# mLSTM attention and mixer on one core: four of twelve spread products move between the heads' products with v

## The chip, the cores and the metric

The kernel runs on one core of a Trainium2 chip. The metric is the device time of one execution in microseconds. The kernel before takes 427.3 us (median of three runs, 426.74 to 427.36).

## The reference

Two parts follow each other. The first is an mLSTM attention for 4 batches, 8 heads, 768 steps, head width 40:

```python
m_new = np.maximum(f_gate[:, :, t] + m, i_gate[:, :, t])
f_stab = np.exp(f_gate[:, :, t] + m - m_new)
i_stab = np.exp(i_gate[:, :, t] - m_new)
C = f_stab * C + i_stab * np.einsum('bhd,bhe->bhde', vt, kt)
n = f_stab * n + i_stab * kt
h_tilde = np.einsum('bhde,bhe->bhd', C, qt)
denom = np.maximum(np.abs((n * qt).sum(-1)), 1.0)
y[:, :, t] = sigmoid(o_gate) * h_tilde / denom
```

The second is a mixer on the heads put side by side (768 tokens of 320 channels in each batch): `h = relu(xT @ w_tok1) @ w_tok2`, `u = x + hT`, and the output is `u + relu(u @ w_ch1) @ w_ch2`, with 256 token units and 1536 channel units. Everything is float32.

## The kernel before, in words

The 768 steps of a batch are cut into 6 chunks of 128. A unit is one chunk of one batch, written (b, c), with all 8 heads. Inside a unit the recurrence is a masked attention: products of q and k (`st_s`, line 313), multiplied on VectorE with a matrix of decays (`st_p`, line 323), then for each head a product with v (`st_pv`, line 439). What came before the chunk enters by the running state (`st_state`, lines 378 and 386). Then the sigmoid gate, the division, and the mixer's matmuls follow.

The matrix of decays is the exponential of phi(t) + b(s), and of a large negative number above the diagonal. Both rows are first computed on VectorE, with one row for each head, in the tile `z` (phi in its first half, b in its second). For the first batch alone, TensorE spreads these rows into full matrices in PSUM, in two halves of four heads. A half is a PSUM bank of 128 x 512 and takes six bf16 products: one 512-column product that writes the mask (`spread_late`, line 165), four 128-column products that spread phi, one for each head (line 180), and one 512-column product that spreads b over the four heads (line 183). The two halves of a unit so hold four long products and eight thin ones. ScalarE then takes the exponential of each half (`prep_exp`, line 291). In bf16 the rows of `z` stand in three parts whose sum is the float32 value. The lower two are made by `split`, two subtractions, for chunks 0 to 2 on VectorE, and for chunks 3 to 5 in one go on GpSimd (lines 174 and 175). Every spread product of a chunk reads all three parts.

The banks come from the PSUM pool `ps_h`, which has two buffers, handed out in turn. A third user of that pool is `spread_q` (line 198, with the two small products of lines 138 and 139): it spreads phi for the scaling of q, and ScalarE reads its bank in `prep_q3` (line 274, an exponential) and right behind it in `cols_w0_out` (line 142).

The loop over the first batch's chunks, c = 1 to 5, is written by hand, and every engine runs its instructions in the order in which they are written. For c up to 3, one turn issues on TensorE: `st_s` of unit c+1, `spread_q` of unit c+1, `st_state` and `st_pv` of unit c, and then the two spread halves of unit c+2. So in each turn `spread_q` takes one buffer of `ps_h`, the first half takes the other, and the second half takes the one that `spread_q` had. On ScalarE one turn issues, among steps that unpack the mixer's weights (lines 684, 654, 658) and a rounded copy of the output (line 490): line 274, line 142, then the two exponentials of line 291. The weights arrive by DMAs that SyncE issues (line 643), between the loads of k and v (line 247) and q (line 258).

The long loops behind it (mixer matmuls of lines 696, 817 and 843, and the attention of batches 1 to 3, which does not spread by TensorE) are left as they are.

Of the kernel before, what the change touches and what calls it, by code (L numbers as in the profile page):

```python
# [17 lines left out]
B, H, S, D = 4, 8, 768, 40  # L18
L = 128
# [16 lines left out]
def kernel(ctx: ExitStack, tc: tile.TileContext, gates, qk, q3, kv, og,  # L36
                            wt1, wt2, wc1, wc2, ident, out):
    nc = tc.nc
# [4 lines left out]
    ps_h = ctx.enter_context(tc.tile_pool(name="ps_h", bufs=2, space=PSUM))  # L43
# [31 lines left out]
    z = pp.tile([128, 2, S], F32, name="z")  # L75
# [23 lines left out]
    id3 = pp.tile([128, HP], BF16, name="id3")  # L99
# [11 lines left out]
    phi, b_t = z[0:B * HP, 0], z[0:B * HP, 1]  # L111
# [51 lines left out]
    def spread_late(pool, tag):  # L163
        ps = pool.tile([128, 4, L], F32, tag=tag, name="ps_phi")
        nc.tensor.matmul(ps, id_b, late_b.unsqueeze(1).to_broadcast([128, 4, L]), start=True, stop=False)
        return ps


    def top(x):
        return x.bitcast(BF16).rearrange("... (t i) -> ... t i", i=2)[..., 1]  # L170
# [6 lines left out]
    def spread_phi(r, c, h0=0, h1=H):  # L177
        zc = top(z[:, :, c * L:(c + 1) * L])
        for h in range(h0, h1):
            nc.tensor.matmul(r[h // 4][:, h % 4, :], id3[:, h:h + 1].to_broadcast([128, 128]),  # L180
                             zc[:, 0], start=False, stop=False)
            if h % 4 == 3:
                nc.tensor.matmul(r[h // 4], zc[:, 1], id3[:, h - 3:h + 1].unsqueeze(2).to_broadcast([128, 4, L]),
                                 start=False, stop=True)

    def spread_split(u, fill=0):
        T[u]["phi"] = r = []
        for h in range(0, H, 4):
            r.append(spread_late(ps_h, "h"))
            if fill and h == 0:  # L190
                warm(fill)
            spread_phi(r, u[1], h, h + 4)

    def spread_q(u, pool=(ps_h, "h")):
        b, c = u
        ps = pool[0].tile([128, 512], F32, tag=pool[1], name="ps_q")
        for g in range(3):
            nc.tensor.matmul(ps[0:120, g * L:(g + 1) * L], sel3[:, g],
                             top(z[:, 0, c * L:(c + 1) * L]), start=True, stop=True)
        T[u]["psq"] = ps[0:120, 0:3 * L].rearrange("p (g t) -> p g t", g=3)  # L200
        if c < NC - 1:
            T[u]["psw"] = ps[:, 3 * L:3 * L + HP]
            cols_w0(T[u]["psw"], c)


    T = {}
# [25 lines left out]
    def load_phi(u):  # L232
        b, c = u
        T.setdefault(u, {})
        third = b < 2 and c % 3 == 2
        dd = ap.tile([128, H, L], F32, tag="p12" if third else "dd", name="dd", bufs=1 if third else 2)
        if b:
            nc.sync.dma_start(out=dd, in_=phi_d[c, b * HP:b * HP + H].partition_broadcast(128))
        T[u]["dd"] = dd
# [67 lines left out]
    def st_s(u, mult=True, mid=iter(()), rows=64, pool=(ps_s, "s")):  # L307
        t = T[u]
        t["s"] = [pool[0].tile([128, 4, L], F32, tag=pool[1], name="ps_sc") for _ in range(2)]
        for h in range(4):  # L310
            for hf in range(2):
                r = t["raw"][64 * hf:64 * hf + rows]
                nc.tensor.matmul(t["s"][hf][:, h, :], r[:, 1, h, :], r[:, 0, h, :], start=True, stop=True)  # L313
        if mult:
            st_p(u, mid)
# [105 lines left out]
        if not joined(u):  # L421
            st_state(u, (ps_s, "s"))

    def st_pv(u, copy=True):
        b, c = u
        t = T[u]
        vx = t["kv"][:, DM:]
        if "p" in t:
            return st_pv3(u)
        if c:  # L430
            po = t["po"]
        else:
            t["bank"] = ps_m.tile([128, 512], F32, tag="m", name="po")
            po = t["bank"][:, 0:H * E1].rearrange("p (h e) -> p h e", e=E1)
        for h in range(H):
            o, x = po[:, h, :], vx[:, h * E1:(h + 1) * E1]
            if b == 0 and c:
                o, x = po[:, 0:h + 2:h + 1, :], x.unsqueeze(1).to_broadcast([128, 2, E1])
            nc.tensor.matmul(o, t["dd"][:, ROW[h], :], x, start=c == 0 and h == 0, stop=h == H - 1)  # L439
        if b == 0 and c:  # L440
            po = po[:, 1:1 + H]
        t["po"] = po
        if b:
            st_ht(u)

    def st_ht(u):
        t = T[u]
        po = t["po"]
        ht = ap.tile([128, H, E1], F32, tag="ht", name="ht", bufs=1)
        nc.scalar.activation(ht, po, AF.Copy)  # L450
        t["ht"] = ht
# [431 lines left out]
    def step(g, n=1):  # L883
        for _ in range(n):
            next(g, None)

    def warm(n, pool=(ps_m, "m"), z=zero):
        t = pool[0].tile([128, 512], F32, tag=pool[1], name="warm")
        for i in range(n):
            nc.tensor.matmul(t[:, 0:z.shape[-1]], z[:, 0:128], z, start=i == 0, stop=i == n - 1)  # L890
# [76 lines left out]
    for c in range(1, NC):  # L967
        u, n1, n2, n3 = (units[c + i] for i in range(4))
        if c == 1:
            st_s(n1)  # L970
        elif c < NC - 1:
            dg = dec_ops(0)
            st_s(n1, mid=dg)
        if c < 3:
            load_phi(n3)
            load_qk(n3, 0)
            load_qk(n3, 1)
        if c == 1:
            dec_load(4)
        if c < NC - 1:  # L980
            spread_q(n1)
            prep_q3(n1)
            prep_kw(n1)
        if c == NC - 2:
            rows_w()
            early[0] = False
            dec_abs(nxt[1] + 2)
        if c == 1:
            dec_abs(2)
        st_state(u)  # L990
        if c == 1:
            dg = dec_ops(0)
        if c < NC - 1:
            step(dg, 2 if c == 1 else 9)
        st_pv(u)
        if c < 4:
            load_kv(n2)
            load_q3(n2)
        dec_load(2 * c + 4)
        x0 = x0_ops(u)  # L1000
        step(x0, 2)
        if c == 2:
            nc.sync.dma_start(out=phi_d.rearrange("c r t -> r c t"), in_=phi.rearrange("p (c t) -> p c t", t=L))
        if c < 4:
            spread_split(n2)
            prep_exp(n2, 0)
            prep_exp(n2, 1)
        if c == NC - 2:
            a_part(0, 0, 0)
            a_part(0, 1, 0)  # L1010
        if c < NC - 1:
            step(dg, 9)
            dec_hi()
            dec_low()
            if c == NC - 2:
                step(x0, 9)
                dec_abs(nxt[1] + 1, (ps_acc, "acc"))
            else:
                dec_abs(nxt[1] + 2)
        step(x0, 9)  # L1020
        if c == NC - 1:
            dec_abs(nxt[1] + 1, (ps_acc, "acc"))
        if c > 3:
            load_sig(1, c - 4)
# [186 lines left out]
```

## Time and profile before

| | |
|---|---|
| median of the runs | 427.3 us |
| the profiled execution's own time | 426.62 us |
| its span, first to last instruction | 424.9 us |
| TensorE busy | 417.8 us, 98% |
| VectorE, ScalarE, GpSimd busy | 66%, 44%, 33% |
| first batch's loop, c = 1 to 3 (TensorE, from `st_pv` of c = 1 to `st_s` behind the spread of c = 3) | 20.64 to 35.94 us |

The profiled execution lies 0.7 us under the median. Times in the trace count from the span's start. In a row of the timeline the first number is the start, the second the length from the first start to the last end; matmuls are pipelined, so the distance of two starts says more of what a matmul costs than its length. Rows of equal instructions are merged, with their count. PEld are TensorE's loads of the stationary operand. A float32 product of a head with v is two passes, so 8 heads are 16 instructions. A bracket at a row's end gives idle time of the engine ahead of it and what ended it.

### The profile page before, as it was taken

Reading aid. Unit: us, or ns where it says so; the run is one execution under the profiler, and the core shown is the slowest. Engines: PE = TensorE matmul, PEld = TensorE weight load, DVE = VectorE, ACT = ScalarE, POOL = GpSimd, SP = SyncE. Lnnn points to the kernel's source line nnn. Section 1 sums busy time; section 2 is a strip of 40 time slices with the busy share of each in tenths; the row PEclk is TensorE's granted clock in tenths of the full one; section 3 lists DMA queues with packets and bytes.
Section 4 is the critical chain, followed back from the end, with each engine's and each line's share of the span. In section 5 each row is a group of like instructions: output and inputs, shape, how many; then the busy total and the mean of one; then the engine's idle time right before and its main releaser. Section 6 shows DMA issues by size and latency. Waiting matters only on the chain.

```text
span 424.9 us, 9011 instructions
## 1 busy us (share of the span) xinstructions
PE 417.8 (98%) x3509; PEld 394.8 (93%) x3510; DVE 280.2 (66%) x624; ACT 188.5 (44%) x438; POOL 141.7 (33%) x184
## 2 busy tenths in 40 slices
PE   7999999999999999999999999999999999999996
PEld 4888989999999999999999999999999999888996
DVE  7988665525777788799796698788886647111412
ACT  5978569883454725334324346335144112111111
POOL 7488488760453501341351230332350110000000
PEclk9999999999999999999999999999999999999999
DMA  7998658940966603434355121433420000000000
GB/s 214 275 283 283 231 174 285 279 150 27 270 203 206 214 34 84 144 117 104 108 162 193 36 95 36 137 118 92 125 86 32 0 22 13 0 2 0 33 30 31
DMA packets 24574, 52.34 MB, mean 123 GB/s; under 512 B 2565, under 2 KB 13325, under 8 KB 24533
## 3 DMA queue, kind: packets, MB, share of 16 engines
q1 hardware_dynamic: 24293, 51.61, 39.3%
q8 instruction: 27, 0.44, 0.4%
q10 hardware_dynamic: 240, 0.18, 0.2%
q14 instruction: 14, 0.11, 0.1%
HBM read 47.73 MB, written 4.04 MB: 122 GB/s over the span
## 4 chain that ended last, share of the span: by engine, by line
PE 93%; POOL 3%; DVE 2%; issue 1%; ACT 1%; POOLq 0%; DVEq 0%
PE acc L696 30%; PE ps_h L817 21%; PE ps_h L843 11%; PE ps_sc L313 5%; PE ps_a L696 5%; PE ps_b L696 5%; PE po L439 4%; PE po L409 3%; PE pu L386 3%; PE po L415 2%; PE po L378 1%; PE ps_h L802 1%; PE ps_phi L180 1%; PE ps_t L767 1%; PE ps_t L765 1%
## 5 line engine op out<-in xcount | busy, mean ns | idle before, releaser
L817 PE MATMUL ps_h<-uT,c1h 128*128 128x256 f32 x480 | 91.7, 282 | 0.3 <-ACT uT L768 0.3
L696 PE MATMUL acc<-c2h,gh 128*128 128x320 f32 x288 | 89.2, 319 | 0.0
L829 ACT ACTIVATE gh<-ps_h 128x512 fp32r<-128x512 f32 x48 | 28.7, 598 | 131.5 <-PE ps_h L817 118.4
L696 PE MATMUL acc<-c2l,gh 128*128 128x320 f32 x288 | 86.3, 309 | 0.0
L817 PEld LDWEIGHTS ps_h<-uT,c1h 128*128 128x128 f32 x480 | 75.8, 188 | 1.3 <-ACT uT L768 0.9
L817 PE MATMUL ps_h<-uT,c1l 128*128 128x256 f32 x256 | 66.0, 280 | 0.0
L830 DVE SCALAR_TENSOR_TENSOR gl<-ps_h,gh 128x512 fp32r<-128x512 f32 x48 | 33.1, 689 | 45.4 <-ACT gh L829 45.3
L696 PE MATMUL acc<-c2h,gl 128*128 128x320 f32 x288 | 61.8, 309 | 0.0
L696 PEld LDWEIGHTS acc<-c2h,gh 128*128 128x128 f32 x288 | 54.1, 188 | 1.6
L696 PEld LDWEIGHTS acc<-c2l,gh 128*128 128x128 f32 x288 | 54.2, 188 | 0.9
L847 DVE SCALAR_TENSOR_TENSOR gl<-ps_h,gh 128x512 fp32r<-128x512 f32 x24 | 16.6, 692 | 48.8 <-ACT gh L846 48.8
L458 POOL TENSOR_TENSOR sig<-sig,ht 128x320 f32<-128x320 f32 x18 | 14.7, 818 | 101.4 <-DVE ht L419 91.3
L817 PEld LDWEIGHTS ps_h<-uT,c1l 128*128 128x128 f32 x256 | 48.2, 188 | 0.0
L696 PEld LDWEIGHTS acc<-c2h,gl 128*128 128x128 f32 x288 | 47.2, 188 | 0.0
L294 ACT ACTIVATE dd<-dd,bcol 128x128 f32<-128x128 f32 x144 | 45.8, 392 | 2.8 <-POOL dd L284 2.7
L843 PE MATMUL ps_h<-uT,c1h 128*128 128x512 f32 x120 | 36.0, 394 | 0.0
L509 POOL TENSOR_TENSOR xl<-x,xh 128x320 fp32r<-128x320 f32 x18 | 15.8, 880 | 51.5 <-DVE xh L507 47.4
L323 DVE TENSOR_TENSOR dd<-ps_sc,dd 128x512 f32<-128x512 f32 x48 | 30.9, 681 | 2.8 <-PE ps_sc L313 2.8
L846 ACT ACTIVATE gh<-ps_h 128x512 fp32r<-128x512 f32 x24 | 14.3, 594 | 41.5 <-PE ps_h L843 41.5
L313 PE MATMUL ps_sc<-raw 64*128 64x128 f32 (+1 forms) x384 | 26.6, 279 | 0.2 <-issue 0.2
L313 PEld LDWEIGHTS ps_sc<-raw 64*128 64x128 f32 (+1 forms) x384 | 23.5, 187 | 2.9 <-issue 2.1
L843 PEld LDWEIGHTS ps_h<-uT,c1h 128*128 128x128 f32 x120 | 22.1, 188 | 3.9
(155 smaller groups left out, 864.9 us busy)
## 6 DMA issues: line engine op xcount, KB each, us to landing
dd<-phi_d SPq DMA_DIRECT2D x18, 512.0 KB
wst<-in_wc_dram SPq DMA_DIRECT2D x22, 384.0 KB
kvt<-in_kv_dram SPq DMA_DIRECT2D x24, 324.0 KB
raw<-in_qk_dram SPq DMA_DIRECT2D x48, 160.0 KB
sig<-in_og_dram SPq DMA_DIRECT2D x8, 480.0 KB
out_dram<-x SPq DMA_DIRECT2D x24, 160.0 KB
q3t<-in_q_dram SPq DMA_DIRECT2D x20, 180.0 KB
wst<-in_wt_dram SPq DMA_DIRECT2D x8, 384.0 KB
```

Of the source, the lines that this page charges most:

```text
L294: nc.scalar.activation(dd[:, h, :], dd[:, h, :], AF.Exp, bias=bcol[:, c, HP * b + h:HP * b + h + 1])
L313: nc.tensor.matmul(t["s"][hf][:, h, :], r[:, 1, h, :], r[:, 0, h, :], start=True, stop=True)
L323: nc.vector.tensor_tensor(dd, t["s"][hf], dd, ALU.mult)
L439: nc.tensor.matmul(o, t["dd"][:, ROW[h], :], x, start=c == 0 and h == 0, stop=h == H - 1)
L458: nc.gpsimd.tensor_tensor(sg, sg, ht[:, :, 0:D], ALU.mult)
L509: nc.gpsimd.tensor_tensor(xl, x, f32(xh), ALU.subtract)
L696: nc.tensor.matmul(ps, a, m, start=(first and i == 0), stop=(last and i == n - 1))
L817: nc.tensor.matmul(ps[:, j, :], c1[x][:, a:a + 128], u[:, y, :], start=not opened and part is first and i == 0 and (order == 0 and not clo ...
L829: nc.scalar.activation(gh, ps, AF.Relu)
L830: nc.vector.scalar_tensor_tensor(gl, ps, 0.0, f32(gh), op0=ALU.max, op1=ALU.subtract)
L843: nc.tensor.matmul(ps, c1[x][:, a:a + 128], u[:, :, y, :], start=n == 0, stop=n == len(todo) - 1)
L847: nc.vector.scalar_tensor_tensor(gl, ps, 0.0, f32(gh), op0=ALU.max, op1=ALU.subtract)
```

## The change

For the first batch, c = 1 to 3, the spread of unit c+2 is split in two parts. The four long products (mask and b, for either half) are issued inside `st_pv` of unit c: one behind each of the heads 0 to 3. The eight thin products, which spread phi, stand where the whole spread stood before, behind `st_pv`. The last thin product of a half now ends the accumulation. Nothing else moves, and the spreads of units 0 to 2, ahead of the loop, are as they were.

```diff
+    def spread_wide(u):
+        T[u]["phi"] = r = []
+        zc = top(z[:, 1, u[1] * L:(u[1] + 1) * L])
+        for h in range(0, H, 4):
+            r.append(spread_late(ps_h, "h"))
+            yield
+            nc.tensor.matmul(r[-1], zc, id3[:, h:h + 4].unsqueeze(2).to_broadcast([128, 4, L]), start=False, stop=False)
+            yield
+
+    def spread_thin(u):
+        zc = top(z[:, 0, u[1] * L:(u[1] + 1) * L])
+        for h in range(H):
+            nc.tensor.matmul(T[u]["phi"][h // 4][:, h % 4, :], id3[:, h:h + 1].to_broadcast([128, 128]),
+                             zc, start=False, stop=h % 4 == 3)
...
-    def st_pv(u, copy=True):
+    def st_pv(u, mid=iter(())):
...
             nc.tensor.matmul(o, t["dd"][:, ROW[h], :], x, start=c == 0 and h == 0, stop=h == H - 1)
+            next(mid, None)
...
-        st_pv(u)
+        st_pv(u, spread_wide(n2) if c < 4 else iter(()))
...
         if c < 4:
-            spread_split(n2)
+            spread_thin(n2)
             prep_exp(n2, 0)
             prep_exp(n2, 1)
```

On TensorE, in the turn c = 1, the products with v of unit (0, 1) and the spread of unit (0, 3) stand so before (`po` is the bank of the products with v, `dd` the decayed scores, `ps_phi` a spread bank, `id_126` and `z` the operands of the spread):

```order
L439 MATMUL po<-kvt,dd 128x82 [waits DVE_49]
L439 MATMUL po<-kvt,dd 128x2x41
L439 MATMUL po<-kvt,dd 128x2x41 [waits DVE_49]
L439 MATMUL po<-kvt,dd 128x2x41 x5
L165 LDWEIGHTS id_b
L165 MATMUL ps_phi<-late_b,id_b 128x512 [waits Activation_49]
L180 LDWEIGHTS id_126
L180 MATMUL ps_phi<-z,id_126 128x128 [waits Pool_49]
```

And so now, at the same place (line 454 is the old 439, line 200 the old 183, line 206 the old 180):

```order
L454 MATMUL po<-kvt,dd 128x82 [waits DVE_49]
L165 LDWEIGHTS id_b
L165 MATMUL ps_phi<-late_b,id_b 128x512 [waits Activation_49]
L454 MATMUL po<-kvt,dd 128x2x41
L200 LDWEIGHTS z [waits Pool_49]
L200 MATMUL ps_phi<-id_126,z 128x512
L454 MATMUL po<-kvt,dd 128x2x41 [waits DVE_49]
L165 LDWEIGHTS id_b [waits PE_49]
L165 MATMUL ps_phi<-late_b,id_b 128x512 [waits Activation_49]
L454 MATMUL po<-kvt,dd 128x2x41
L200 LDWEIGHTS z
L200 MATMUL ps_phi<-id_126,z 128x512
```

The wait on GpSimd, which stood ahead of the first thin product behind all eight heads, stands now ahead of the second long one, with six heads behind it. The wait on ScalarE for the second buffer, which stood behind the whole first half, stands now ahead of the third long product, with five heads behind it.

In the turns c = 2 and 3 TensorE has before, behind the eight heads, the first half of the spread and then the second:

```order
L439 MATMUL po<-kvt,dd 128x2x41 x7
L165 LDWEIGHTS id_b
L165 MATMUL ps_phi<-late_b,id_b 128x512 [waits Activation_49]
...
L183 LDWEIGHTS z
L183 MATMUL ps_phi<-id_126,z 128x512
L165 LDWEIGHTS id_b [waits PE_49]
L165 MATMUL ps_phi<-late_b,id_b 128x512 [waits Activation_49]
```

and now:

```order
L454 MATMUL po<-kvt,dd 128x2x41
L165 LDWEIGHTS id_b [waits PE_49]
L165 MATMUL ps_phi<-late_b,id_b 128x512 [waits Activation_49]
L454 MATMUL po<-kvt,dd 128x2x41
L200 LDWEIGHTS z
L200 MATMUL ps_phi<-id_126,z 128x512
L454 MATMUL po<-kvt,dd 128x2x41 x4
L206 LDWEIGHTS id_126
L206 MATMUL ps_phi<-z,id_126 128x128
```

Here the second half's mask product, which takes the buffer that `spread_q` had in the same turn, comes ahead of five heads instead of behind all eight and a half spread. The instructions of VectorE, ScalarE, GpSimd and SyncE stand in the same order as before.

## Rows read from the trace of the kernel before

**Rows 1.** The page, part 1: busy time, share of the span, instructions.
```profile
PE 417.8 (98%) x3509; PEld 394.8 (93%) x3510; DVE 280.2 (66%) x624; ACT 188.5 (44%) x438; POOL 141.7 (33%) x184
```

**Rows 2.** TensorE's waits in all: us, times, longest; behind 42 us this alone.
```profile
PE ps_h L817 <- ACT uT L768: 0.3, 2, 0.2
```

**Rows 3.** Busy time by window: TensorE, its loads, VectorE, ScalarE, GpSimd, clock, DMA share.
```profile
45.00:125.00 80.00, 79.83 (x558) 73.78 (x558) 46.13 (x103) 52.12 (x122) 44.26 (x58) 1.00 0.62 196
```

**Rows 4.** Timeline of TensorE, turn c = 2: start, length, line, tiles, count.
```profile
26.74 0.23 PE L386 MATMUL pu<-kvt,kw 128*80 128x82 f32 x1
26.81 1.95 PE L439 MATMUL po<-kvt,dd 128*128 128x82 f32 x16
28.59 0.38 PE L165 MATMUL ps_phi<-late_b,id_b 128*128 128x512 bf16 x1
28.81 0.39 PE L180 MATMUL ps_phi<-z,id 128*128 128x128 bf16 x4
29.04 0.38 PE L183 MATMUL ps_phi<-id,z 128*128 128x512 bf16 x1
...
29.70 0.38 PE L183 MATMUL ps_phi<-id,z 128*128 128x512 bf16 x1
30.01 1.16 PE L313 MATMUL ps_sc<-raw 64*128 64x128 f32 x16
```

**Rows 5.** Timeline of TensorE's loads, turn c = 2, under the first mask product.
```profile
28.60 0.10 PEld L180 LDWEIGHTS <-id 128*128 128x128 bf16 x1
```

**Rows 6.** Timeline of GpSimd, turn c = 1: the two steps of `split` for chunks 3 to 5.
```profile
19.82 1.46 POOL L174 TENSOR_TENSOR z<-z 9x768 f32<-9x768 f32 x1
21.36 1.46 POOL L175 TENSOR_TENSOR z<-z 9x768 f32<-9x768 f32 x1
```

**Rows 7.** Timeline of TensorE, turn c = 1.
```profile
20.64 1.95 PE L439 MATMUL po<-kvt,dd 128*128 128x82 f32 x16
22.43 0.38 PE L165 MATMUL ps_phi<-late_b,id_b 128*128 128x512 bf16 x1
22.88 0.39 PE L180 MATMUL ps_phi<-z,id 128*128 128x128 bf16 x4
...
24.07 1.16 PE L313 MATMUL ps_sc<-raw 64*128 64x128 f32 x16
```

**Rows 8.** Timeline of ScalarE, turns c = 2 to 4, of its unbroken queue the ends.
```profile
27.26 0.52 ACT L654 ACTIVATE pf<-wst 128x384 f32<-128x384 f32 x1 [0.35 <-DMA wst<-in_wt_dram]
...
28.98 0.17 ACT L142 ACTIVATE wcol<-ps_q 128x9 f32<-128x9 f32 x1
29.45 1.26 ACT L291 ACTIVATE dd<-ps_phi 128x512 f32<-128x512 f32 x2 [0.30 <-PE ps_phi L183]
30.61 0.93 ACT L684 ACTIVATE w1h<-wf 128x384 fp32r<-128x384 f32 x2
...
34.13 0.17 ACT L142 ACTIVATE wcol<-ps_q 128x9 f32<-128x9 f32 x1
...
36.54 0.93 ACT L684 ACTIVATE w2h<-wf 128x384 fp32r<-128x384 f32 x2
...
39.71 0.46 ACT L274 ACTIVATE pq<-ps_q 120x384 f32<-120x384 f32 x1
```

**Rows 9.** Timeline of TensorE, turn c = 3.
```profile
32.74 1.95 PE L439 MATMUL po<-kvt,dd 128*128 128x82 f32 x16
...
35.94 1.16 PE L313 MATMUL ps_sc<-raw 64*128 64x128 f32 x16
```

**Rows 10.** Timeline of GpSimd behind the spreads, turn c = 4.
```profile
40.70 1.02 POOL L280 TENSOR_TENSOR q3t<-q3t,pq 120x384 f32<-120x384 f32 x1
```

**Rows 11.** Timeline of TensorE, start of turn c = 5.
```profile
41.77 0.95 PE L378 MATMUL po<-Cn,q3t 120*128 120x164 f32 x6 [0.31 <-POOL q3t L280]
```

**Rows 12.** Timeline of TensorE, the warm-up products at the kernel's start.
```profile
1.39 4.24 PE L890 MATMUL warm<-zero 128*128 128x512 bf16 x10 [1.39 <-POOL zero L61]
```

**Rows 13.** Waits of SyncE's DMA queue, 30 to 40 us: total, times, longest.
```profile
SPq L247 <- PE po L439: 4.8, 1, 4.8
```

## The prediction

> **What bounds the kernel now.** I read the engines' shares first: TensorE is busy for 98% of the span, and so are its loads for 93%, while ScalarE stands at 44% and GpSimd at 33% [rows 1]. Those shares hold for the whole kernel, so next comes the stage. TensorE's waits and the windows behind the first batch's loop show that there is nearly nothing in which a later start could be made up: 0.3 us of waits behind 42 us in all [rows 2], and 79.83 us busy in an 80 us window [rows 3]. So a microsecond that TensorE loses in the loop is a microsecond of the kernel, and one that it gains as well, unless another engine holds the loop. Then the timelines of the loop, of TensorE and of whom it waits for: the reader is to see that TensorE runs almost without a gap there, but that two of the things it needs come late, just before it asks for them in today's order. GpSimd ends the split of z for chunks 3 to 5 at 22.82 us [rows 6], and ScalarE ends reading the bank of `spread_q` in turn c = 2 at 29.15 us [rows 8].
>
> **What the interleaving gives by itself.** The 16 passes of the eight heads take 1.78 us, from 26.81 to 28.59, or 0.111 each; a long product takes 0.215 (28.59 to 28.81), a thin one 0.058 (four from 28.81 to 29.04) [rows 4]. A pass has only 82 columns to stream. Behind a product whose load was short (80 columns of weights, line 386) a pass of 82 columns is followed after 0.07 us by the next product, 26.74 to 26.81 [rows 4]. So a head's pass is held by its own load, 128 columns of float32, and not by its stream. Under a long product the next load is done in advance: the load for the first thin product begins at 28.60 [rows 5], and that product starts at 28.81, as soon as the long one's 0.215 are over [rows 4]. A head behind a long product thus finds its first load done; its second load then starts with its first pass, and the second pass follows after about 0.07 instead of 0.111. Each of the 12 moved products so gives 0.04 us. The bounds: 0 if nothing is hidden, and 0.111 if a whole load vanishes, 1.3 us in all. I take 0.04, the value next to the row with the 0.07: 0.17 us for each turn and 0.5 us for three, if nothing waits.
>
> The Trainium skill's page "TensorE: Matmul & The Clock Gate" (section The mechanism) says that a load overlaps a running matmul only where the two use different rows of the array. By that the long products would hide nothing, and the 0.5 us would be 0. The trace does not bear it out here: both instructions use all 128 rows, and the load at 28.60 was hidden [rows 4, 5].
>
> **The wait on GpSimd, turn c = 1.** Now the second long product, behind head 1, is the first to read z of chunk 3. TensorE comes to it at 20.64 [rows 7] + 0.22 (head 0) + 0.215 (mask) + 0.18 (head 1: 0.07 and 0.11) = 21.26. GpSimd is done at 21.36 + 1.46 = 22.82 [rows 6], and its queue ahead of that does not hang on this change. Before, the thin product followed 0.05 after that end (22.88 [rows 7]), with its load done; now the load waits too, so the product starts at 22.82 + 0.05 + 0.07 = 22.94. The stall is 1.68 us, where before it was 0.23 (22.43 + 0.215 to 22.88). Behind the waiting product stand on TensorE's queue six heads, which need nothing of it, two long products and all eight thin ones. From 22.94: long 0.215, head 0.18, long 0.215, head 0.18, long 0.215, then eight passes 0.07 + 7 x 0.111, the eighth interval ending at the first thin product: 24.80. Eight thin ones, the last starting 0.41 later, and `st_s` 0.15 behind that start (before, it started 0.07 ahead of the recorded end of the last spread product, 29.70 + 0.38 against 30.01 [rows 4]; a thin one is recorded for 0.22): 25.35 instead of 24.07 [rows 7]. Loss so far 1.28 us.
>
> The Trainium skill says in the same section that matmuls start and end strictly in program order. By that nothing passes a waiting product, which is what the sum takes; if heads could pass it, the third rival's result would come out. No row here shows a matmul overtaking another.
>
> **The wait on ScalarE, turns c = 2 and 3.** The third long product takes the bank of `spread_q`, and must wait until ScalarE has done lines 274 and 142. These stand on ScalarE's queue behind the last turn's two exponentials and seven more steps. Without waits that queue takes, from the first exponential to the end of line 142: 0.50 + 0.50 (two exponentials; from the second, 29.45 + 1.26 - 0.60, to 30.61), then 34.13 - 30.61 = 3.52, then 0.17: 4.69 us [rows 8]. And the first exponential needs the first half's last thin product, which now stands behind all heads. It starts 0.25 after that product's start (0.22 recorded, and 0.03 as before between 29.04 + 0.38 [rows 4] and 29.45 [rows 8]).
>
> Turn c = 1: that thin product starts at 24.80 + 0.17 = 24.97, the exponential at 25.22, line 142 ends at 29.91. The DMA for which ScalarE waited before came at 27.26 [rows 8] and hangs on no engine of this chain; ScalarE reaches that step now at about 28.0. Turn c = 2: TensorE comes to the third long product at 26.81 [rows 4] + 1.28 + 1.01 (0.22 + 0.215 + 0.18 + 0.215 + 0.18) = 29.10 and waits until 29.97. From there: long 0.215, head 0.18, long 0.215, eight passes 0.85, three thin 0.17, so the fourth thin product at 31.60, the exponential at 31.86 (before 29.45) and `st_s` at 31.99 (before 30.01 [rows 4]): loss 1.98. Turn c = 3: line 142 ends at 31.86 + 4.69 = 36.55, the product starts at 36.61; TensorE was there at 32.74 [rows 9] + 1.98 + 1.01 = 35.73. `st_s` comes 2.02 later, at 38.63 instead of 35.94 [rows 9]: loss 2.69. TensorE and ScalarE now go in a ring whose period is 1.89 + 4.69 + 0.06 = 6.64 us, against 5.94 of a turn before.
>
> **The end of the loop.** Turn c = 4 has no spread, but line 378 of turn c = 5 waits for q scaled by GpSimd, which follows line 274, and it waited 0.31 us already [rows 11]. The exponential of turn c = 3 starts at 36.61 + 1.89 = 38.50; line 274 follows after 1.00 + 3.17 (36.54 to 39.71 [rows 8]) at 42.67, 2.96 later than before. GpSimd's scaling (40.70 [rows 10]) and line 378 (41.77 [rows 11]) move by the same. TensorE alone would be there 2.69 - 0.31 = 2.38 late, so this chain ends last. The sum is 2.95 us lost. Behind it nothing gives it back [rows 2, 3].
>
> The profiled execution took 426.62 us, so it would come to 429.6; its median of runs lies 0.7 us higher, at 427.3, and I forecast 430.2.
>
> **Rivals.**
> - *Only the GpSimd wait costs.* The turns c = 2 and 3 do not stall, and each gives its 0.17: 1.28 - 0.34 = 0.94 us, 428.2. For it: before, ScalarE idled 0.30 us ahead of c = 2's exponentials [rows 8], so its queue is not full. Against: in turn c = 2 the bank was read at 28.98 to 29.15 even in the undisturbed order [rows 8], 1.3 us behind the point to which the product moves (27.82).
> - *Slower still, by late loads.* SyncE issues the load of k and v for unit (0, 5) only when the heads of c = 3 are done [rows 13], and the weights' DMAs stand behind it on its queue. These heads end about 3.5 us later (37.96 against 34.42 for the last pass), 0.6 us more than the rest. If the weights' unpacking hangs on them at once, 3.6 us are lost: 430.9.
> - *No wait binds, and the hiding is seen.* The time is 426.8 (-0.5), and 426.0 if whole loads vanish (-1.3). For it: the row with 0.07, and TensorE's 98%. Against: both waits are in the written order, in front of products that cannot be done without what they wait for. This is the one case on the other side: it decides if GpSimd ended its split before 21.26 and ScalarE its queue before 29.10.
> - *The clock.* The warm-up products took 0.41 us each at the start, (5.47 - 1.39)/10, where a long product takes 0.215 [rows 4, 12]. If TensorE falls back to the lower of its two clocks (1.2 instead of 2.4 GHz) behind a stall, 3 us of work at half speed cost 3 us more: 433. Against: the granted clock stays at 1.00 [rows 3], and the pause of 0.31 us [rows 11] does not show in it; but the new stall of 1.68 us is over five times as long.
>
> **How the numbers follow.** Forecast 0.78, only GpSimd 0.07, late loads 0.05, the clock 0.04, no wait 0.06 (of it 0.02 with more than 0.2%). A measurement can tell about 0.2% from no change, 0.85 us. The first, third and fourth cases are slower, and most of the second, whose 0.94 us stand just over that line: slower 0.91, same 0.07, faster 0.02. The range, 428.1 to 431.3 us, reaches from just under the case with only GpSimd to the late loads with 0.4 us for the spread of the runs; the clock and the last case are left out.
>
> **What would show it.** In turn c = 1, a gap on TensorE from about 21.3 to 22.9, ended by GpSimd's line 175; in c = 2 and 3, gaps of some 0.9 us ahead of the third long product, ended by ScalarE's line 142; `st_s` at 25.35, 31.99 and 38.63; line 378 of c = 5 at 44.7, waiting for GpSimd; and all behind it later by the same. Passes at 0.07 behind long products would show the hiding. If the second long product starts before 22.8, or the chain behind c = 3 is late by less than 2 us, the forecast fails.

## The result, and the profile after

| kernel | median of runs, us | lowest to highest | ratio to before (95%) |
|---|---|---|---|
| before | 427.26 (6 runs) | 426.62 to 427.37 | |
| changed | 430.19 (6 runs) | 428.81 to 431.43 | 1.0078 (1.0064 to 1.0092) |

The change costs 2.9 us by the medians; the ratio in the table is 3.3 us, its interval 2.7 to 3.9. The profiled execution of the changed kernel took 431.27 us, with a span of 429.3. Its loop begins 0.14 us earlier than that of before (the heads of c = 1 at 20.50 instead of 20.64 [rows 7]), so 0.14 is taken off wherever a time of the prediction stands beside one of this profile. The line numbers differ: the moved and the thin products of the first batch's turns, before in lines 183 and 180, stand in lines 200 and 206 (the mask stays in 165); 274 is 289, 280 is 295, 291 is 306, 313 is 328, 378 is 393, 439 is 454.

First TensorE's waits from 20 to 60 us: the waiting line, what it waited for, us in all, times, longest.

```profile
PE ps_phi L200 <- POOL z L175: 1.5, 1, 1.5
PE ps_a L712 <- POOL xl L507: 1.4, 1, 1.4
PE ps_phi L165 <- ACT wcol L142: 1.4, 2, 0.7
PE po L393 <- POOL q3t L295: 0.5, 1, 0.5
```

The first, third and fourth are the waits of the forecast, with the releasers that it named. The second is not of the loop; it comes at 51.54 us. Now the places themselves, on TensorE's timeline: start, length, line, tiles, count, idle time before.

```profile
20.50 0.39 PE L454 MATMUL po<-kvt,dd 128*128 128x82 f32 x2
20.72 0.38 PE L165 MATMUL ps_phi<-late_b,id_b 128*128 128x512 bf16 x1
20.94 0.34 PE L454 MATMUL po<-kvt,dd 128*128 128x82 f32 x2
22.74 0.39 PE L200 MATMUL ps_phi<-id,z 128*128 128x512 bf16 x1 [1.46 <-POOL z L175]
22.97 0.35 PE L454 MATMUL po<-kvt,dd 128*128 128x82 f32 x2
...
24.62 0.62 PE L206 MATMUL ps_phi<-z,id 128*128 128x128 bf16 x8
...
28.34 0.34 PE L454 MATMUL po<-kvt,dd 128*128 128x82 f32 x2
28.53 0.38 PE L200 MATMUL ps_phi<-id,z 128*128 128x512 bf16 x1
28.74 0.34 PE L454 MATMUL po<-kvt,dd 128*128 128x82 f32 x2
29.75 0.38 PE L165 MATMUL ps_phi<-late_b,id_b 128*128 128x512 bf16 x1 [0.67 <-ACT wcol L142]
...
36.38 0.38 PE L165 MATMUL ps_phi<-late_b,id_b 128*128 128x512 bf16 x1 [0.69 <-ACT wcol L142]
...
38.39 1.16 PE L328 MATMUL ps_sc<-raw 64*128 64x128 f32 x16
...
44.44 0.95 PE L393 MATMUL po<-Cn,q3t 120*128 120x164 f32 x6 [0.54 <-POOL q3t L295]
...
51.54 0.41 PE L712 MATMUL ps_a<-xl,w1h 128*128 128x320 f32 x1 [1.39 <-POOL xl L507]
```

The idle time in brackets counts from the recorded end of the product before, which lies behind the point where the next could start. The stall is better read from start to start: a head in front of a long product takes 0.18 or 0.19 (28.34 to 28.53), so the second long product of c = 1 was due at 20.94 + 0.18 = 21.12 and lost 1.62; the third of c = 2 was due at 28.74 + 0.18 = 28.92 and lost 0.83; that of c = 3 lost 0.86.

The other two engines, on their timelines: the end of GpSimd's `split`, and of ScalarE's queue the reading of the bank, the exponentials, line 289, and two conversions of weights behind it.

```profile
21.22 1.46 POOL L175 TENSOR_TENSOR z<-z 9x768 f32<-9x768 f32 x1
```
```profile
25.05 1.08 ACT L306 ACTIVATE dd<-ps_phi 128x512 f32<-128x512 f32 x2 [3.24 <-PE ps_phi L206]
...
29.54 0.16 ACT L142 ACTIVATE wcol<-ps_q 128x9 f32<-128x9 f32 x1
31.65 1.08 ACT L306 ACTIVATE dd<-ps_phi 128x512 f32<-128x512 f32 x2 [1.94 <-PE ps_phi L206]
...
36.14 0.18 ACT L142 ACTIVATE wcol<-ps_q 128x9 f32<-128x9 f32 x1
38.27 1.08 ACT L306 ACTIVATE dd<-ps_phi 128x512 f32<-128x512 f32 x2 [1.94 <-PE ps_phi L206]
...
42.38 0.48 ACT L289 ACTIVATE pq<-ps_q 120x384 f32<-120x384 f32 x1
43.52 0.52 ACT L670 ACTIVATE pf<-wst 128x384 f32<-128x384 f32 x1 [0.66 <-DMA wst<-in_wc_dram]
46.86 0.52 ACT L670 ACTIVATE pf<-wst 128x384 f32<-128x384 f32 x1 [2.82 <-DMA wst<-in_wc_dram]
```

GpSimd ends at 22.68, and the waiting product starts 0.06 later. ScalarE now idles 1.94 us ahead of the exponentials of c = 2 and 3, where before it idled 0.30 [rows 8] and 1.08, and then TensorE waits for ScalarE: the ring, with a period of 36.38 - 29.75 = 6.63 us.

From the start of the heads of c = 1 to line 378 (now 393) of c = 5, which I call the loop, it takes 21.13 us before (41.77 - 20.64 [rows 7, 11]) and 23.94 after: 2.81 us more. From there to the first product of line 843, which I call the tail, this profile takes 16.45 us, where before took 14.79. These further 1.66 us hold the wait of 1.39 at 51.54. On ScalarE two conversions wait for a DMA with weights ahead of that, until 43.52 and until 46.86. That both belong together is argued from the order of the queues, not shown; the first experiment asks whether the change causes it.

### The profile page after: what moved, and what is told of

It reads as the page before. It is cut to its first block, busy times and chain, and to the rows that moved or that the text cites. A ratio compares the mean times of both kernels' runs of the same rounds, so it can differ in the third digit from the quotient of the medians.

```text
span 429.3 us, 9012 instructions
## 1 busy us (share of the span) xinstructions
PE 418.7 (98%) x3510; PEld 395.9 (92%) x3510; DVE 281.8 (66%) x624; ACT 187.8 (44%) x438; POOL 142.8 (33%) x184
## 4 chain that ended last, share of the span: by engine, by line
PE 87%; ACT 6%; DMA 3%; POOL 2%; issue 1%; DVE 0%; SPq 0%; POOLq 0%; DVEq 0%; ACTq 0%
PE acc L712 29%; PE ps_h L833 20%; PE ps_h L859 10%; PE ps_b L712 5%; PE ps_a L712 4%; PE ps_sc L328 4%; PE po L454 3%; PE po L424 3%; PE pu L401 2%; DMA wst<-in_wc_dram 2%; PE po L430 2%; DMA dd<-phi_d 2%; PE warm L906 1%; ACT dd L306 1%; PE po L393 1%; ACT wst L674 1%
## 5 line engine op out<-in xcount | busy, mean ns | idle before, releaser
L833 PEld LDWEIGHTS ps_h<-uT,c1h 128*128 128x128 f32 x480 | 75.8, 188 | 1.3 <-ACT uT L784 0.9
L454 PEld LDWEIGHTS po<-kvt,dd 128*128 128x128 f32 x192 | 24.3, 192 | 2.0 <-issue 1.6
```

Source lines behind the costliest of these rows:

```text
L833: nc.tensor.matmul(ps[:, j, :], c1[x][:, a:a + 128], u[:, y, :], start=not opened and part is first and i == 0 and (order == 0 and not clo ...
```

## The experiments

For each kernel the loop and the tail of its profile, and its times beside those of the kernel before on the same chip (medians 427.26 for the changed kernel, 426.76 for `again`, `late_half`, `best` and `ctl_split3`, 426.8 for the others).

| kernel | loop, us | tail, us | median, us | ratio (95%) |
|---|---|---|---|---|
| before | 21.13 | 14.79 | | |
| changed | 23.94 | 16.45 | 430.19 | 1.0078 (1.0064 to 1.0092) |
| again | 23.95 | 14.78 | 429.94 | 1.0075 (1.0057 to 1.0092) |
| only_c1 | 22.32 | 14.80 | 428.0 | 1.0027 (1.0017 to 1.0037) |
| only_c23 | 23.36 | 15.69 | 429.43 | 1.0061 (1.004 to 1.0083) |
| first_half | 20.93 | 14.80 | 426.91 | 1.0009 (0.9997 to 1.0021) |
| late_half | 21.12 | 14.80 | 426.98 | 1.0003 (0.9993 to 1.0013) |
| load_first | 23.97 | 14.78 | 430.04 | 1.0075 (1.0061 to 1.0089) |
| split3 | 22.32 | 15.32 | 428.68 | 1.0051 (1.0031 to 1.0071) |
| act_order | 24.56 | 14.76 | 430.1 | 1.0081 (1.0066 to 1.0096) |
| both | 23.51 | 14.77 | 429.15 | 1.0054 (1.0038 to 1.007) |
| ctl | 22.81 | 14.76 | 428.99 | 1.0055 (1.0042 to 1.0069) |
| best | 20.99 | 15.79 | 426.83 | 1.0001 (0.9991 to 1.0012) |
| ctl_split3 | 21.15 | 14.79 | 426.78 | 0.9997 (0.9988 to 1.0005) |

**again.** The changed kernel, unaltered, for a second profile and further times.

> The whole change once more, unaltered, for a second profile beside these. Theory of the two waits with late loads: the same three gaps (1.5, 0.7, 0.7 us) and 2.8 us lost up to line 378 of turn c = 5; the wait of 1.4 us for GpSimd near 50 us is there only if the weights land late again. 430.0. Rival (that wait belongs to the change as much as the gaps): the same 1.4 us in this profile.

Measured: 429.94 us, and a profile of 430.2 us whose loop takes 23.95 and whose tail takes 14.78. Line 393 of c = 5 waits as before, and the conversion that had waited 2.82 us for a DMA now waits for VectorE. It starts 1.32 earlier by the clock, and 1.64 counted from the loop's start, which lies at 20.82 here. TensorE and ScalarE, timelines:

```profile
44.77 0.95 PE L393 MATMUL po<-Cn,q3t 120*128 120x164 f32 x6 [0.55 <-POOL q3t L295]
```
```profile
45.54 0.52 ACT L670 ACTIVATE pf<-wst 128x384 f32<-128x384 f32 x1 [1.70 <-DVE po L497]
```

So the loop's 2.8 us come back to a hundredth, and the 1.66 us of the tail do not belong to every execution. SyncE issued these weights equally late in both: at 38.97 in the first profile and 39.28 in this one, 18.47 and 18.46 us behind the loop's start.

**only_c1 and only_c23: which wait costs what.** The products are moved in turn c = 1 alone, or in c = 2 and 3 alone.

```diff
-        st_pv(u, spread_wide(n2) if c < 4 else iter(()))
+        st_pv(u, spread_wide(n2) if c == 1 else iter(()))   # only_c23: c in (2, 3)
...
-            spread_thin(n2)
+            (spread_thin if c == 1 else spread_split)(n2)   # only_c23: c in (2, 3)
```

> The long products stand between the heads in turn c = 1 alone; turns c = 2 and 3 spread as before. Theory (a wait on GpSimd in c = 1 and a wait on ScalarE in c = 2 and 3 make the loss): the gap on TensorE before the second long product of c = 1 stays, about 1.5 us, the other two gaps are gone, and all behind is later by that alone: 1.3 us more than before, 428.5 us. Rival (mixing bf16 and float32 products costs by itself, the same in each turn): a third of the 2.9 us, 1.0 us, with passes slower than 0.111 us. Rival (the ScalarE waits are all): no loss, 427.2.

> The long products stand between the heads in turns c = 2 and 3; turn c = 1 spreads as before. Theory: no wait on GpSimd beyond the 0.2 us of before, but ScalarE's queue reaches line 142 at about 29.1 us as before and TensorE asks at 27.8, so the gap of c = 2 grows from 0.7 to about 1.2 us, and c = 3 waits in the ring of 6.6 us a turn: 2.2 us more than before, 429.5; the two single losses then add to more than the whole change's. Rival (only the wait on GpSimd costs): 0.3 us less than before, 426.9. Rival (mixing itself costs): 2 us, without gaps.

Measured: with c = 1 alone the loop is 1.19 us longer and the time 1.2 us; its profile has no other new wait than the one on GpSimd. With c = 2 and 3 alone the loop is 2.23 longer and the time 2.6 (the tail of this profile is 0.90 longer too). Without the loss of c = 1, TensorE comes to the third long product of c = 2 on time, but ScalarE, which on its way waits 0.39 and 0.27 us for DMAs of weights, ends line 142 only at 29.43, and the idle time is twice that of the whole change. TensorE and ScalarE of only_c23, timelines:

```profile
29.48 0.38 PE L165 MATMUL ps_phi<-late_b,id_b 128*128 128x512 bf16 x1 [1.30 <-ACT wcol L142]
```
```profile
29.25 0.18 ACT L142 ACTIVATE wcol<-ps_q 128x9 f32<-128x9 f32 x1
```

The parts sum to 1.19 + 2.23 = 3.42, more than the 2.81 of the whole. That is what a chain through one bank gives: a TensorE that is late already waits less for ScalarE.

**first_half and late_half: is it the place between the heads, or the bank?** In both, turn c = 1 is as before, and c = 2 and 3 move products. In first_half only the two long ones of the first half move; the second half, with the bank of `spread_q`, stays behind the heads. In late_half all four move, but the second pair stands behind heads 6 and 7. Both also carry the edit of only_c23.

```diff
# first_half
-        for h in range(0, H, 4):
+        for h in range(0, 4, 4):
...
-        for h in range(H):
+        for h in range(4):
...
+        r = T[u]["phi"]
+        r.append(spread_late(ps_h, "h"))
+        spread_phi(r, u[1], 4, H)
# late_half, in spread_wide
         for h in range(0, H, 4):
+            if h:
+                for _ in range(4):
+                    yield
```

> In turns c = 2 and 3 only the first half's two long products stand between the heads; the second half's stand behind as before, and turn c = 1 is as before. Neither of the two waits is moved. Theory: no new gap, each of the four moved products gives 0.04 us, 0.17 us less than before in all: 427.1, no measurable change. Rival (mixing bf16 and float32 products costs by itself): four of twelve products, 1.0 us more, 428.2.

> In turns c = 2 and 3 all four long products stand between the heads, but the second half's two behind heads 6 and 7 instead of 2 and 3; turn c = 1 is as before. Theory (the point at which TensorE asks for the bank, against ScalarE's line 142, sets the price): in c = 2 TensorE asks at about 28.7 us instead of 27.8 and waits 0.5 us, in c = 3 it hardly waits; 0.4 to 0.5 us more than before, 427.3, of the 2.6 that the same products cost behind heads 2 and 3. Rival (the mixing costs by itself, or the last thin product's place behind all heads makes the ring): the same 2.6 us, 429.4.

Measured: neither time can be told from before. So the switch between bf16 and float32 products costs nothing that shows, and the place at which TensorE asks for the bank is what costs. In late_half I had expected 0.4 to 0.5 us of loss. The interval of its ratio, up to 1.0013, would still hold that; its profile does not show it. There ScalarE waited for no DMA of weights, had read the bank at 28.38, and the product came at 28.73 without a wait. TensorE and ScalarE of late_half, timelines (its lines are 3 higher):

```profile
28.73 0.38 PE L165 MATMUL ps_phi<-late_b,id_b 128*128 128x512 bf16 x1
...
38.35 1.95 PE L457 MATMUL po<-kvt,dd 128*128 128x82 f32 x16
...
41.77 0.95 PE L396 MATMUL po<-Cn,q3t 120*128 120x164 f32 x6 [0.55 <-POOL q3t L298]
```
```profile
28.21 0.17 ACT L142 ACTIVATE wcol<-ps_q 128x9 f32<-128x9 f32 x1
...
39.71 0.47 ACT L292 ACTIVATE pq<-ps_q 120x384 f32<-120x384 f32 x1
```

This pair also shows what becomes of a gain. From the heads of c = 1 to those of c = 4 TensorE takes 38.35 - 20.65 = 17.70 us where before took 17.95 (38.59 - 20.64). That is 0.25 for eight moved products, of which six have a head right behind them (the last one of a turn is followed by a thin product): 0.04 for each of the six. Then line 378's product waits 0.55 instead of 0.31 [rows 11] and starts at 41.77, as before. Line 274 on ScalarE starts at 39.71 in both [rows 8], and GpSimd's scaling hangs on it. TensorE's gain ends in the wait for that chain.

The chain itself starts on TensorE: the exponentials of c = 3 need the first half's last thin product. In late_half that product stands behind all heads and all four long products, so the exponentials start later than before although TensorE is ahead. In first_half it stands behind two long ones only. ScalarE of before, late_half and first_half, timelines, and TensorE of first_half:

```profile
35.39 1.26 ACT L291 ACTIVATE dd<-ps_phi 128x512 f32<-128x512 f32 x2 [1.08 <-PE ps_phi L183]
```
```profile
35.58 1.08 ACT L309 ACTIVATE dd<-ps_phi 128x512 f32<-128x512 f32 x2 [1.14 <-PE ps_phi L209]
```
```profile
34.83 1.25 ACT L309 ACTIVATE dd<-ps_phi 128x512 f32<-128x512 f32 x2 [0.99 <-PE ps_phi L206]
```
```profile
41.21 0.95 PE L396 MATMUL po<-Cn,q3t 120*128 120x164 f32 x6 [0.31 <-POOL q3t L298]
```

Counted from the loop's start (20.64, 20.65 and 20.28) the exponentials start at 14.75, 14.93 and 14.55. So in first_half the chain moves with TensorE, and its loop is 0.20 us shorter with the same wait of 0.31 at the end. The times of the runs cannot tell 0.2 us.

**load_first: are late weights part of the cost?** In turn c = 3 the weights' DMA is issued ahead of the loads of k and v, for which SyncE waits until the heads are done.

```diff
+        if c == 3:
+            dec_load(2 * c + 4)
         if c < 4:
             load_kv(n2)
```

> The whole change, but in turn c = 3 SyncE issues the two weight loads ahead of the load of k and v, which waits for that turn's heads, instead of behind it. Theory with late loads (part of the loss, 0 to 1.5 us from run to run, comes from weights that land late at 43 to 47 us): ScalarE's waits for the weights (0.7 and 2.8 us) and TensorE's wait of 1.4 us for GpSimd at 50 us go; the loop's loss of 2.8 us stays: 429.5 to 430.0, with less spread than 428.8 to 431.4. Rival (the loop's waits are all, late loads cost nothing): as the whole change, 430.2, with the same spread.

Measured: in its profile SyncE issues these loads at 30.78, ScalarE converts both without a wait, and the tail takes 14.78. SyncE's DMA queue and ScalarE, timelines:

```profile
30.78 1.44 SPq L659 DMA_DIRECT2D wst<-in_wc_dram  x2
```
```profile
43.00 0.95 ACT L670 ACTIVATE pf<-wst 128x384 f32<-128x384 f32 x2
```

The median stays: 1.0075. So late weights are no measurable part of the median's 2.9 us. That the edit took the wait away is not shown, as `again` was without it too. Whether late weights explain the spread upward is left open: the runs still lie between 428.98 and 430.79.

**split3, act_order, both, ctl: take the waits away.** split3 lets GpSimd split chunk 3 first and chunks 4 and 5 behind it. act_order takes a weight unpacking off ScalarE's queue ahead of line 142 and puts it behind. both does the two, and ctl does the two on the kernel before.

```diff
# split3
-    split(3, NC, nc.gpsimd)
+    split(3, 4, nc.gpsimd)
+    split(4, NC, nc.gpsimd)
# act_order
-            st_s(n1, mid=dg)
+            st_s(n1, mult=False)
...
             prep_kw(n1)
+        if 1 < c < NC - 1:
+            dec_abs(nxt[1] + 2)
+            st_p(n1, dg)
...
-            else:
-                dec_abs(nxt[1] + 2)
```

> The whole change, and GpSimd splits z of chunk 3 first (128 columns) and of chunks 4 and 5 behind it, instead of all three in one go. Theory of the two waits: the gap of 1.5 us before the second long product of c = 1 goes, ScalarE's gaps stay and the first of them grows; the loss is that of the change in c = 2 and 3 alone, less the 0.2 us for which TensorE waited on GpSimd before: 2.0 to 2.4 us, 428.8 to 429.2. Rival (only the wait on GpSimd costs): 0.5 to 0.7 us less than before, 426.2.

> The whole change, and on ScalarE the four steps that unpack weights stand behind lines 274 and 142 (old numbers) of the turn instead of ahead of them; VectorE, GpSimd and SyncE keep their order. Theory of the two waits: ScalarE is done with the bank about 2 us sooner, the gaps of c = 2 and 3 go, the one of c = 1 stays; line 378 of turn c = 5 no longer waits for GpSimd. Loss 0.6 to 0.9 us, 427.4 to 427.7. Rival (the waits of c = 2 and 3 come from something else, as from TensorE's own products): gaps of 0.7 us stay, 430.

> The whole change with both of these edits. Theory of the two waits: no gap is left in the loop; what the moved products hide is seen alone, 0.5 us, and with the 0.2 and 0.3 us of waits that the kernel before has in the loop the time is about 1.0 us less than before: 425.8. Rival (mixing costs by itself): over 427. Rival (nothing is hidden): equal to the control.

> The control: the kernel before, with the spread behind the heads, and both edits (chunk 3 split first on GpSimd, the unpacking behind lines 274 and 142 on ScalarE). Theory: it loses the 0.2 and 0.3 us of waits, 426.3, and the difference to the whole change with both edits is what the moved products hide, 0.5 us. Rival (nothing is hidden): no difference between the two.

Measured: split3 does what it should. GpSimd has chunk 3 at 20.67 + 0.61 = 21.28, the second long product starts at 21.43 without a wait, and the loop is 1.6 us shorter than the change's. ScalarE's waits are left, the first at only 0.27, since ScalarE waited for no DMA ahead of it in this profile; I had expected it to grow. Part of what the split saves comes back one turn later, as ctl_split3 will show. GpSimd and TensorE of split3, timelines:

```profile
20.67 0.61 POOL L175 TENSOR_TENSOR z<-z 9x256 f32<-9x256 f32 x1
```
```profile
21.43 0.38 PE L200 MATMUL ps_phi<-id,z 128*128 128x512 bf16 x1
...
28.44 0.38 PE L165 MATMUL ps_phi<-late_b,id_b 128*128 128x512 bf16 x1 [0.27 <-ACT wcol L142]
...
35.04 0.38 PE L165 MATMUL ps_phi<-late_b,id_b 128*128 128x512 bf16 x1 [0.68 <-ACT wcol L142]
```

act_order takes ScalarE's waits away: the third long product of c = 2 starts at 29.16, right behind its head. But the time is no better than that of the change, 430.1 us where I had expected 427.4 to 427.7. ctl shows why: the two edits by themselves cost 2.2 us on the kernel before, and split3's edit alone costs nothing there (ctl_split3, below). TensorE of act_order and of ctl, timelines:

```profile
28.98 0.34 PE L454 MATMUL po<-kvt,dd 128*128 128x82 f32 x2
29.16 0.38 PE L165 MATMUL ps_phi<-late_b,id_b 128*128 128x512 bf16 x1
...
45.30 0.92 PE L393 MATMUL po<-Cn,q3t 120*128 120x164 f32 x6 [1.21 <-DVE Cn L410]
```
```profile
43.54 0.92 PE L378 MATMUL po<-Cn,q3t 120*128 120x164 f32 x6 [1.20 <-DVE Cn L395]
```

VectorE, timeline of ctl:

```profile
40.72 0.56 DVE L672 SCALAR_TENSOR_TENSOR wf<-pf,wst 128x384 int32<-128x384 int32 x1 [1.39 <-POOL xl L491]
```

In both kernels line 378's product waits 1.2 us for VectorE's update of the state. VectorE's queue holds the unpacking of the weights (line 672) ahead of it, and that step comes later: it idled 1.39 us before it. The bracket names GpSimd's line 491, which ended at 40.19; ScalarE's part of the unpacking (line 658) ended at 40.63, right ahead of the 40.72. That this part is what held the step is read from these two ends, not tested. There are further new waits, on GpSimd, at the state's product of line 386 (401): 0.38 and 0.85 us in act_order, 0.60 and 0.86 in both, 0.57 in ctl. So the experiment exchanged one wait for another, and says of ScalarE only that its waits can be removed, not what that is worth. The expectations of both (425.8) and ctl (426.3) missed by 3.35 and 2.69 us, with these same waits in their profiles. With the two edits the change makes no difference that the runs can tell (429.15 against 428.99); in the profiles its loop is 0.70 us longer, 23.51 against 22.81. Its 0.5 us are not seen there either.

**best and ctl_split3: is there a version that beats both?** best has split3, all four products moved in c = 1, and of c = 2 and 3 only the first half. ctl_split3 is the kernel before with split3.

```diff
...
-        st_pv(u, spread_wide(n2) if c < 4 else iter(()))
+        st_pv(u, spread_wide(n2, H if c == 1 else 4) if c < 4 else iter(()))
...
```

> GpSimd splits z of chunk 3 first; turn c = 1 has all four long products between the heads, turns c = 2 and 3 the first half's two alone, the second half behind the heads as before. No wait is moved to where it binds. Theory: TensorE gains 0.2 (wait on GpSimd) + 0.17 + 0.08 + 0.08 = 0.5 us in the loop: 426.3, if the other engines let it through. Rival (VectorE and ScalarE hold the loop as tightly as TensorE, as the reordering runs suggest): TensorE waits for them instead, 426.8.

> The control to it: the kernel before, with chunk 3 split first on GpSimd and nothing else. Theory: the 0.2 us wait of c = 1 goes, 426.6, and 0.3 us lie between this and the one with the moved products. Rival: the wait returns at the next product, 426.8.

Measured: 426.83 and 426.78 against 426.76; no version beats the kernel before. In ctl_split3 the old pause of c = 1, 0.23 us, is gone: the thin products start 0.22 behind the mask. In best the waits that the change brought are gone. The time stays in both, and in best line 378's product of c = 5 still waits 0.30 us for GpSimd, as before. TensorE of ctl_split3 and of best (its lines are 4 higher than the change's), timelines:

```profile
22.47 0.38 PE L165 MATMUL ps_phi<-late_b,id_b 128*128 128x512 bf16 x1
22.69 0.39 PE L180 MATMUL ps_phi<-z,id 128*128 128x128 bf16 x4
```
```profile
25.54 0.95 PE L397 MATMUL po<-Cn,q3t 120*128 120x164 f32 x6 [0.24 <-POOL q3t L299]
...
41.75 0.95 PE L397 MATMUL po<-Cn,q3t 120*128 120x164 f32 x6 [0.30 <-POOL q3t L299]
```

The first of these two lines shows where the gain of c = 1 goes: best has a new wait for GpSimd, at line 378's product of c = 2. Four steps of `split` take GpSimd 3.52 us (19.86 to 23.38 in ctl_split3), where two took 3.00 [rows 6], and the scaling of q stands behind them. GpSimd of before and of ctl_split3, timelines:

```profile
23.86 0.99 POOL L280 TENSOR_TENSOR q3t<-q3t,pq 120x384 f32<-120x384 f32 x1
```
```profile
24.40 1.01 POOL L280 TENSOR_TENSOR q3t<-q3t,pq 120x384 f32<-120x384 f32 x1
```

In ctl_split3 the scaling comes 0.54 later, 0.50 counted from the loop's start. `st_s` of c = 1 comes 0.23 sooner by the same count (23.88 instead of 24.07 [rows 7], from 20.68), but line 378's product of c = 2 starts at 4.79 instead of 4.80. The second expectation's rival came true: the wait returned further down.

## Why the prediction was right, step by step

| step | forecast (clock times less 0.14) | measured |
|---|---|---|
| c = 1, second long product starts | 22.80 | 22.74 |
| c = 1, `st_s` | 25.21 | 25.17 |
| c = 2, third long product | 29.83 | 29.75 |
| c = 2, `st_s` | 31.85 | 31.77 |
| period of the ring | 6.64 | 6.63 |
| c = 3, third long product | 36.47 | 36.38 |
| c = 3, `st_s` | 38.49 | 38.39 |
| line 274 (289), c = 4 | 42.53 | 42.38 |
| line 378 (393), c = 5 | 44.59 | 44.44 |
| loss in the loop | 2.95 | 2.81 |

- *The hiding.* The passes of a head between long products follow as forecast: a head there takes 0.18, where two passes took 0.22 before (1.78/8 [rows 4]). The pair of a head behind a long product is recorded over 0.34 us (20.94), that of head 0, which has none ahead, over 0.39 (20.50), so the second pass starts 0.05 sooner. The first load of such a head starts with the long product, here the one of 28.13. TensorE's loads of the changed kernel, timeline:

```profile
28.13 0.41 PEld L454 LDWEIGHTS po<-kvt,dd 128*128 128x128 f32 x2
```

Of the 0.5 us that "nothing waits" would have given, late_half shows 0.25 for its six heads behind long products, against 0.24 by the forecast's 0.04. What the third rival left out is the end of the loop: line 378 of c = 5 waits for a chain through ScalarE and GpSimd that starts at the first half's last thin product, and with all four long products moved this product comes later within its turn. In late_half nothing of the gain arrives; in first_half, where only two move, 0.20 us arrive (0.04 of them from c = 1, where GpSimd was done a little sooner). So the rival asked too much even where the two waits are gone: late_half and best are not faster than before.

By the sentence that the prediction draws from the Trainium skill, "TensorE: Matmul & The Clock Gate", section The mechanism, taken alone, the heads between long products would have stayed at 0.22. The trace of after disagrees here too: 0.18. The same section also lets a load into a background weight buffer go ahead of running matmuls, which the prediction did not weigh; with that the 0.18 is no contradiction, though no trace here shows which buffer a load goes to.

- *The wait on GpSimd* came where it should, and only_c1 and split3 show it as cause: alone it costs 1.19 us in the loop, against the 1.28 forecast, and with the split done in time the wait at this place vanishes. One term was too large: the 0.07 for the waiting product's load. The product is recorded at 22.74, at the same time as its load, 0.06 behind GpSimd's end. The prediction named a start before 22.8 as a sign against it, and 22.74 is before that by the clock. But this profile's loop begins 0.14 sooner: the product starts 2.24 us behind the loop's start, in `again` too (23.06 - 20.82), where the sign is 2.16 (22.8 - 20.64).
- *The wait on ScalarE* came in both turns, and its ring has the period that was summed from ScalarE's queue. only_c23 shows it as cause: 2.23 us in the loop by itself, so the rival that only GpSimd's wait costs falls. That best, which leaves the bank of `spread_q` behind the heads, loses nothing shows the same from the other side; the attempt to free ScalarE instead, act_order, is no evidence of a size. How long the first of the two waits is depends on what else is late. In the change TensorE comes late itself and ScalarE's queue runs unbroken: 0.67. In only_c23 TensorE is on time and ScalarE waits for DMAs of weights: 1.30. In split3 TensorE is on time and ScalarE waits for none: 0.27.
- *The end.* Line 378 of c = 5 waits for GpSimd at 44.44, and in `again` all behind it is later by the loop's loss. The median of runs is 2.93 us higher, the sum was 2.95. That they agree to 0.02 is luck: the loop's loss is 2.81, single runs lie 2.6 us apart, and the profiled execution, for which 429.6 was forecast, took 431.27 with its late wait.
- *Late loads* were given 0.05. In one of two profiles of the change they cost 1.66 us on top, in the other nothing, and the medians fit the loop without them. The rival's reason, that SyncE issues the weights later, does not decide it: the two profiles of the change have them issued equally late, and one waits. In best SyncE issues them at 36.09, near the 35.66 of before, and ScalarE still waits 1.15 and 1.67 us for them. How often such waits come, and whether the change makes them likelier, stays open: in the profiles of split3, only_c23 and best the same product waits too, 0.26, 0.65 and 0.74 us, and best, whose profiled execution is the longest of its runs, is in the median not slower than before.
- *The clock* stayed up. After the stalls the window of 45 to 125 us (columns as in [rows 3]) reads:

```profile
45.00:125.00 80.00, 78.44 (x539) 72.47 (x539) 43.86 (x95) 53.04 (x123) 44.84 (x57) 1.00 0.63 203
```

The granted clock is 1.00, and the 1.39 us that TensorE lacks against [rows 3] are as long as the late wait at 51.54. The 3 us of work at half speed, by which the prediction priced this rival, came from no row, and no run here tests them.

## What to carry to other kernels

Here the moved instructions cost TensorE not their length but the waits that they brought. Before moving one ahead on an engine that runs its queue in order, read from the trace when each of its inputs and its buffer come free, and set that beside the time at which the engine would arrive. Ask the same of a gain: here late_half's 0.25 us on TensorE ended in the wait for a chain through two engines that are busy less than half of the time, because the same move put the start of that chain later. Where a shared bank closes a ring between two engines, sum the ring's period from the other engine's queue; that gave 6.64 us against 6.63 measured.

## What the runs showed of the hardware

- A head's two passes take 0.18 us from start to start behind a 512-column product and 0.22 elsewhere, and the first of its two loads starts with that product (28.13).
- A product that waited for another engine is recorded at 22.74, together with the load of its own weights, 0.06 us behind the writer's end; the 0.10 of that load did not come on top.
- Of two profiles of the same program one has a conversion that waits 2.82 us for a DMA of weights and a TensorE pause of 1.39 us later, the other neither. The weights' DMAs were issued 18.47 and 18.46 us behind the loop's start, so the time of issue does not tell the two apart. One profile is not enough to count such a pause as a cost of the change.
